# Loading the first columns of a weight from the scalar queue, and scheduling the output projection further behind its transposes

## The chip, the core and the metric

The kernel runs on one core of one Trainium2 chip. The metric is device time in microseconds (us), taken as the median of the runs. The profiled span is about 1.75 us shorter than the device time of the same execution (153.8 against 155.57), so spans are compared with spans only. Every timed run was also listed with its span and its granted TensorE clock: the share of full speed at which TensorE was allowed to run, averaged over the run.

A ratio below is the mean time of one kernel's fast runs over the mean of the other kernel's fast runs in the same rounds, so it is not quite the ratio of the medians that are quoted.

## The reference, cut to what matters

```python
xn = layernorm(x)                        # x: 1 x 2048 x 448, bf16
h  = silu(xn @ w1)                       # w1: 448 x 1792
ff = h @ w2                              # w2: 1792 x 448
q, k, v = split(xn @ wqkv)               # 16 heads of 28
# phi_q, phi_k: softmax of +/- (q @ w_phi), 56 features a head
o  = (phi_q @ (phi_k.T @ v)) / den
return x + o @ wo + ff
```

The kernel works on 16 tiles of 128 rows. At the start it needs a tile of `x`, its layer norm, its transpose, and the first columns of `w1`. At the end it needs the attention output `o` of each tile, transposed by a DMA, as the stationary operand of the product with `wo`.

## The kernel before: the parts that matter

Every operation is recorded first. A list scheduler in the kernel's Python then fixes the order on each engine, from modelled durations. Two kinds of numbers only steer that order: `lat` of a load, and `slack`, which makes an operation count as ready later than its inputs. Neither makes the chip wait. What the chip waits for are semaphores.

```python
            for d in o.deps:
                dd = ops[d]
                t = max(t, dd.end + lat(dd, o) + (o.slack if dd.eng != o.eng else 0.0))
```

The loads. All but `Wp` stand in the sync queue, in this order:

```python
        load(Wp[:], A_w_phi.rearrange("(g hl) d f -> (hl d) g f", g=G), "wphi", eng="act", lat=3000.0)
        load_x(0, 1)
        load_x(1, 2)
        load_x(2, 4)
        load_w1(0, 512, 3200.0)
        load_w1(512, 1024, 3200.0)
        load_x(4, 8)
        load_w1(1024, FF)
```

`load_w1` makes two transfers: 384 rows (384 KB for 512 columns, called the first piece of w1 below) and the last 128 rows (128 KB).

The first four tiles are normalized on VectorE and transposed by TensorE. Fixed chains keep their order:

```python
        chain("bnst0 bnag0 bnst1 bnag1 rstd0 xn0 rstd1 xn1 bnst2 bnag2 bnst3 bnag3 rstd2 xn2 rstd3 xn3 ev3".split())
        chain("ev0 ve2 ev1 ve3 ev2 silu_table".split())
        chain("tr0 tr1 tr2 tr3".split())
        # [...]
        for t, fs in ((0, head[:2]), (1, head[:2]), (0, head[2:3]), (1, head[2:3]), (2, head[:3]), (3, head[:3])):
            for f in fs:
                f[0](True, t * 128, t * 128 + 128)
```

`xn0`, tile 0's normalization, stands behind `bnst1`, the statistics of tile 1. `ev1`, ScalarE's copy of tile 1's transpose, stands behind `ve2`, tile 2's square root. So tile 1's operand waits for the load of tiles 2 and 3.

The end of the kernel:

```python
        def wo_fulls(q, ob, cs, st):
            P.cur_slack = 900.0
            for n in range(3):
                mm(ob, oT_sb[:, q, n + q % 2, :], wo_sb[:, q % 2, n, cs], st and n == 0, False, "wo_mm")
            P.cur_slack = 0.0
```

The softmax here doesn't subtract the row's maximum and nothing guards it: scores larger than these inputs give would overflow.

## Time and profile before

| | before |
|---|---|
| median of the first 3 runs | 153.57 us (153.53 to 153.88) |
| the profiled execution itself | 155.57 us, span 153.8 us, mean granted clock 0.989 |
| TensorE busy | 148.2 us, 96% of the span |

The profile is of an execution 2.0 us longer than the median.

The page of the kernel before: the span, the busy time of TensorE, its busy tenths in 40 slices and its granted clock in tenths.

```profile
span 153.8 us, 2800 instructions
PE 148.2 (96%) x1118; PEld 79.4 (52%) x1118; DVE 90.0 (59%) x171; ACT 72.6 (47%) x86; POOL 67.4 (44%) x76
PE   7599999999999999999999999999999999999993
PEclk9959999999999999999999999999999999999999
```

TensorE is full from the third slice on, but in that slice the clock was at half.

The chain of work that ended last in before, in order of time (start us, duration us, what; PE is TensorE, and L438 is the line of the helper through which its matmuls go):

```profile
2.20 5.12 DMA phT<-in_B_w_dram
7.32 0.14 issue
7.45 1.93 PE psum L438 x19
...
10.87 86.31 PE psum L438 x653
...
118.81 4.37 DMA vaug<-vaug
...
123.23 28.00 PE psum L438 x215
```

Read backwards, this execution hangs on TensorE, then on one transposed attention output (`vaug`), then on TensorE, and at the start on the first piece of w1, which is stored under the name `phT`: issued 2.20, landed 7.32.

The timeline of before at both places (start us, duration us, engine, line, what, and in brackets the idle time before it and what ended that):

```profile
3.87 0.59 DVE L563 BATCH_NORM_STATS2 st<-x_sb 128x6 f32<-128x448 bf16 x1
...
5.73 0.60 ACT L458 ACTIVATE xnT<-psum 128x512 bf16<-128x512 bf16 x1 [0.71 <-PE psum L453]
...
7.38 0.58 ACT L458 ACTIVATE xnT<-psum 128x512 bf16<-128x512 bf16 x1
...
7.45 1.93 PE L438 MATMUL psum<-xnT,phT 128*128 128x128 bf16 x19 [1.33 <-DMA phT<-in_B_w_dram]
...
123.23 0.74 PE L438 MATMUL psum<-wo_sb,vaug 128*128 128x448 bf16 x3 [0.22 <-DMA vaug<-vaug]
```

The first line is tile 1's statistics, the next two are the copies of tiles 0 and 1. Both copies were done before or soon after the first feed-forward matmul: only w1 was late.

### The profile page before, as it was taken

What the parts mean: (1) busy time and instruction counts of PE and PEld (TensorE: products, weight loads), DVE (VectorE), ACT (ScalarE), POOL (GpSimd) and SP (SyncE); (2) the same over time, 40 slices, a digit from 0 to 9 for tenths busy, and PEclk for the clock granted to TensorE, in tenths of its full rate; (3) what the DMA queues carried; (4) which work ended last, traced back from release to release, by engine and by line L of the source; (5) the groups of instructions that cost most, each with busy time, mean ns of one, the idle gap of its engine ahead of it and who ended that gap; (6) DMA issues with size and microseconds to landing.
All of it is one profiled execution on the core that took longest, in us unless ns stands there. A gap on an engine that the chain in (4) does not pass through costs nothing.

```text
span 153.8 us, 2800 instructions
## 1 busy us (share of the span) xinstructions
PE 148.2 (96%) x1118; PEld 79.4 (52%) x1118; DVE 90.0 (59%) x171; ACT 72.6 (47%) x86; POOL 67.4 (44%) x76
## 2 busy tenths in 40 slices
PE   7599999999999999999999999999999999999993
PEld 7497444446444556545434444445554455555482
DVE  1748888306019998897112521999973724474552
ACT  3452884676688669698555759784000000000000
POOL 7105564300014999999993000499997000000000
PEclk9959999999999999999999999999999999999999
DMA  5997554799940000000058311065899993144151
GB/s 90 320 387 285 112 105 81 91 240 280 238 137 0 4 0 0 9 0 0 4 114 161 66 34 38 0 122 98 171 124 191 207 199 68 39 124 124 36 155 64
DMA packets 44206, 17.38 MB, mean 113 GB/s; under 512 B 36640, under 2 KB 43808, under 8 KB 44192
## 3 DMA queue, kind: packets, MB, share of 16 engines
q1 hardware_dynamic: 41568, 15.44, 45.3%
q10 hardware_dynamic: 2624, 1.75, 3.8%
q8 instruction: 9, 0.15, 0.4%
q14 instruction: 5, 0.04, 0.1%
HBM read 6.56 MB, written 1.84 MB: 55 GB/s over the span
## 4 chain that ended last, share of the span: by engine, by line
PE 91%; DMA 6%; SPq 1%; issue 0%; DVE 0%
PE psum L438 90%; DMA phT<-in_B_w_dram 3%; DMA vaug<-vaug 3%; SPq L499 1%; PE psum L453 1%; DVE x_sb L776 0%
## 5 line engine op out<-in xcount | busy, mean ns | idle before, releaser
L438 PE MATMUL psum<-xnT,phT 128*128 128x512 bf16 (+2 forms) x278 | 49.2, 346 | 1.3 <-DMA phT<-in_B_w_dram 1.3
L438 PE MATMUL psum<-w_sb,hT 128*128 128x448 bf16 (+1 forms) x238 | 48.6, 342 | 0.0
L458 ACT ACTIVATE hT<-psum 128x1024 bf16<-128x1024 f32 x28 | 27.9, 1025 | 18.8 <-PE psum L438 18.8
L706 POOL TENSOR_TENSOR RA<-Ek_sb,Rec 128x896 bf16<-128x896 bf16 x16 | 26.6, 1700 | 16.3 <-DVE Rec L674 16.3
L438 PEld LDWEIGHTS psum<-xnT,phT 128*128 128x128 bf16 (+1 forms) x278 | 21.1, 102 | 21.6 <-issue 4.7
L438 PEld LDWEIGHTS psum<-w_sb,hT 128*128 128x128 bf16 x238 | 22.2, 98 | 17.4 <-issue 0.6
L673 DVE TENSOR_REDUCE Rec<-Ek_sb 128x64 f32<-128x1792 bf16 x12 | 23.7, 1978 | 12.0 <-ACT Ek_sb L458 12.0
L458 ACT ACTIVATE Ek_sb<-psum 128x896 bf16<-128x896 f32 x24 | 20.4, 927 | 5.0 <-PE psum L438 2.3
L681 POOL TENSOR_TENSOR Ek_sb<-Ek_sb,Rec 128x896 bf16<-128x896 bf16 x8 | 13.3, 1698 | 5.7 <-DVE Rec L674 5.6
L753 DVE TENSOR_SCALAR den<-psum 128x16 f32<-128x16 f32 x16 | 2.7, 171 | 19.6 <-PE psum L438 19.6
L438 PE MATMUL psum<-wv,xnT 128*128 128x448 bf16 (+1 forms) x64 | 13.5, 352 | 0.0
L438 PE MATMUL psum<-Wk,xnT 128*128 128x448 bf16 (+1 forms) x64 | 13.5, 353 | 0.0
L681 POOL TENSOR_TENSOR phT<-phT,Rec 128x896 bf16<-128x896 bf16 x8 | 13.3, 1706 | 0.0
L438 PE MATMUL psum<-Wq,xnT 128*128 128x448 bf16 (+1 forms) x64 | 12.5, 353 | 0.0
L438 PE MATMUL psum<-wo_sb,vaug 128*128 128x448 bf16 (+1 forms) x51 | 11.7, 342 | 0.2 <-DMA vaug<-vaug 0.2
L563 DVE BATCH_NORM_STATS2 st<-x_sb 128x6 f32<-128x448 bf16 x16 | 9.6, 602 | 3.7 <-DMA x_sb<-in_A_x_dram 3.7
L776 DVE TENSOR_TENSOR x_sb<-psum,x_sb 128x448 bf16<-128x448 f32 (+1 forms) x13 | 7.1, 583 | 5.9 <-PE psum L438 5.8
L760 DVE TENSOR_TENSOR vaug<-psum,rden 128x448 bf16<-128x448 f32 x16 | 10.0, 624 | 0.8 <-DVE rden L755 0.2
L578 DVE TENSOR_SCALAR RA<-x_sb,mv,rstd 128x384 bf16<-128x384 bf16 (+2 forms) x28 | 8.8, 350 | 2.7 <-POOL rstd L574 2.6
L674 DVE RECIPROCAL Rec<-Rec 128x64 f32<-128x64 f32 x16 | 8.7, 546 | 0.3
L673 DVE TENSOR_REDUCE Rec<-phT 128x64 f32<-128x1792 bf16 x4 | 8.0, 1990 | 0.9 <-ACT phT L458 0.9
L572 POOL TENSOR_SCALAR ve<-mv 128x1 f32<-128x1 f32 x12 | 2.6, 217 | 13.2 <-DVE mv L564 13.2
(49 smaller groups left out, 118.2 us busy)
## 6 DMA issues: line engine op xcount, KB each, us to landing
out_dram<-x_sb ACTq DMA_DIRECT2D x15, 112.0 KB, 2.6
w_sb<-in_B_w_dram SPq DMA_DIRECT2D x1, 1568.0 KB, 8.0
x_sb<-in_A_x_dram SPq DMA_DIRECT2D x3, 448.0 KB, 7.4
phT<-in_B_w_dram SPq DMA_DIRECT2D x2, 384.0 KB, 5.3
wo_sb<-in_A_wo_dram SPq DMA_DIRECT2D x2, 336.0 KB, 4.0
phT<-in_B_w_dram SPq DMA_DIRECT2D x1, 576.0 KB, 7.1
wv<-in_A_wqkv_dram SPq DMA_DIRECT2D x1, 336.0 KB, 7.2
phT<-in_B_w_dram SPq DMA_DIRECT2D x2, 128.0 KB, 5.2
```

Of the source, the lines that this page charges most:

```text
L438: r = e.matmul(dst, lhsT, rhs, start=st, stop=sp, skip_group_check=True)
L458: P.op("act", d_act(n), lambda e: e.activation(dst, src, func, scale=scale), reads=[src], writes=[dst], table=table, name=name, **keys)
L563: P.op("dve", 590, lambda e: e.bn_stats(st6[:, t, :], xs), reads=[xs], writes=[st6[:, t, :]], name=f"bnst{t}", okeys_w=["ln"])
L572: P.op("pool", 200, lambda e: e.tensor_scalar(ve[:, t:t + 1], mv[:, t, 1:2], EPS_LN, None, ALU.add), reads=[mv[:, t, 1:2]], writes=[ve[:, ...
L578: P.op("dve", dur, lambda e: e.tensor_scalar(dst, x_sb[:, t, c0:c1], mv[:, t, 0:1], rstd[:, t:t + 1], ALU.subtract, ALU.mult), reads=[xs, ...
L673: P.op("dve", 1985, lambda e: e.tensor_reduce(R2, E4, AXL.X, ALU.add), reads=[E4], writes=[R2], name="Ssum")
L674: P.op("dve", 555, lambda e: e.reciprocal(R2, R2), reads=[R2], writes=[R2], name="Rrec")
L681: P.op("pool", 1700, lambda e: e.tensor_tensor(E3, E3, Rk[:, :, None].broadcast_to([128, 32, DH]), ALU.mult), reads=[E3, Rk], writes=[E3], ...
L706: P.op("pool", 1700, lambda e: e.tensor_tensor(dst, Eq, Rq.rearrange("p (c j) -> p c j", c=CC)[:, :, :, None].broadcast_to([128, CC, 4, DH ...
L753: P.op("dve", 190, lambda e: e.tensor_scalar(den[:, uq, :], U3[:, :, DH], EPS_DEN, None, ALU.add), reads=[U3[:, :, DH]], writes=[den[:, uq ...
L760: P.op("dve", 620, lambda e: e.tensor_tensor(o3, U3[:, :, 0:DH], rden[:, uq, :, None].broadcast_to([128, H, DH]), ALU.mult), reads=[U3[:, ...
L776: P.op("dve", d_dve(cs.stop - cs.start), lambda e: e.tensor_tensor(res[:, cs], ob, addend[:, cs], ALU.add), reads=[ob, addend[:, cs]], wri ...
```

## The change

Its intent is to let TensorE start earlier, by issuing the first 512 columns of w1 from the otherwise idle scalar queue, and to keep TensorE from reaching a `wo` product before its transposed operand has landed.

```diff
+        load_w1(0, 512, 2000.0, "act")
         load_x(2, 4)
-        load_w1(0, 512, 3200.0)
-        load_w1(512, 1024, 3200.0)
+        load_w1(512, 1024, 2500.0)
         load_x(4, 8)
[... load_rows4 and load_w1 pass eng on ...]
         def wo_fulls(q, ob, cs, st):
-            P.cur_slack = 900.0
+            P.cur_slack = 1500.0
[... the same in finish_tile ...]
```

On TensorE the static order changes in two separate places. In the head, 9 instead of 6 feed-forward matmuls stand before tile 3's transposes. After 116 us, `wo` products stand behind more `w2` products.

More of the change, by code (lines that the diff above doesn't have):

```diff
@@ L502, in load_x, with load_rows4, load_w1 @@
             load(x_sb[:, t0:t1, :], xt[:, t0:t1, :], f"x{t0}")
-        def load_rows4(dst, src, c0, c1, name, lat=1700.0):
-            load(dst[:, 0:3, :], src[0:KF, c0:c1].rearrange("(k p) f -> p k f", p=128), name, lat=lat)
-            load(dst[:, 3, :], src[D - 128:D, c0:c1], name, lat=lat)
-        def load_w1(c0, c1, lat=1700.0):
-            load_rows4(w1_sb[:, :, c0:c1], B_w1, c0, c1, "w1", lat)
+        def load_rows4(dst, src, c0, c1, name, lat=1700.0, eng="sp"):
+            load(dst[:, 0:3, :], src[0:KF, c0:c1].rearrange("(k p) f -> p k f", p=128), name, lat=lat, eng=eng)
+            load(dst[:, 3, :], src[D - 128:D, c0:c1], name, lat=lat, eng=eng)
+        def load_w1(c0, c1, lat=1700.0, eng="sp"):
+            load_rows4(w1_sb[:, :, c0:c1], B_w1, c0, c1, "w1", lat, eng)
         load(Wp[:], A_w_phi.rearrange("(g hl) d f -> (hl d) g f", g=G), "wphi", eng="act", lat=3000.0)
@@ L790, in finish_tile @@
                 wo_fulls(q, ob, cs, t < NYT)
-                P.cur_slack = 900.0
+                P.cur_slack = 1500.0
                 pe_mms([wo_rem(q, ob, slice(0, 128), cs)], "wo_mm")
```

## The prediction

> **What bounds it now.** TensorE. The page gives PE 148.2 us busy of a 153.8 us span; the chain of waits puts 90% on the matmul helper and ends in matmuls from 7.45 us to 151.23 us, then one addition and one store. So only time before 7.45 us, and TensorE gaps after it, can be won.
>
> The head, from the timeline: warm-up matmuls end at 4.9, the transposes of tiles 0 and 1 at 6.12, then TensorE idles 1.33 us until the first w1 piece (issued 2.20, landed 7.32) lets the feed-forward start at 7.45. Tile 0's operand was ready at 6.33. The narrow windows show the clock at 1.0 until 7.75, at 0.5 from 7.75 to about 11.2, then 1.0: 7 to 8 matmuls per 0.5 us when slow, 13 afterwards. The Trainium skill, "TensorE: Matmul & The Clock Gate" (HAM clock gate), says that a too idle window of about 3.4 us halves the clock for the next; this trace agrees (3.41 us at 0.5 after that gap).
>
> Near the end the waits show one stall on the transposed attention output: at 123.23 TensorE starts about 0.4 us later than the 0.19 us spacing of its neighbours would have it.
>
> **What the change does.** It adds and removes no work. (1) The first 512 columns of w1 (384 + 128 KB) leave the sync queue (issued 2.20 and 2.68) for the scalar queue, behind w_phi's issue, which ended at 1.22; I expect 1.25 to 2.1, about 0.95 us earlier. (A 1.28 us table load on ScalarE starts there too; I expect the issue not to wait for its end.) Everything behind on the sync queue is issued 0.9 to 1.0 us earlier. (2) New latencies and a larger slack reorder the static schedule: wo's products wait 0.6 us longer in the model.
>
> **How much is on the critical path.** Not 0.95 us. The skill, "DMA: Bandwidth & Descriptors" (Issuing engines are not separate DMA queues), says that a second issuer saves only issue time, since all share the same 16 engines. From 4.5 us on they carry 300 to 400 GB/s here; between 3.0 and 4.5 us only 72 to 222, which the earlier issue can fill. But w1 now shares with x tiles 2 and 3 (landed 6.27) and the next w1 piece instead of following alone. I estimate the first piece at 6.7 (6.2 to 7.3), x tiles 2 and 3 unchanged or up to 0.3 late.
>
> Then a second gate shows. Tile 1's copy on ScalarE stands behind tile 2's square root, which waits for x tiles 2 and 3: it ran 7.38 to 7.96. Tile 0's 12 matmuls would be done by about 7.6, and tile 1's start near 8.2 instead of 8.65. Gain 0.2 to 0.6 us. If the added work before 7.75 us keeps the clock at full speed (30%), about 1 us more. The slack removes up to 0.4 us near 123 us, less what the new order costs elsewhere; I count 0.2.
>
> **Predicted time.** 152.8 us, 151.8 to 153.6 (8 in 10): 0.5% faster. Over 2% faster: 3%; within 2%: 95%; over 2% slower: 2%.
>
> **What would show it.** Right: two w1 issues on the scalar queue before 2.2 us; first feed-forward matmul between 6.4 and 7.2, then a short gap before tile 1; later stages shifted by the same amount, equal in length; no wait on the transposed output near 123 us. The clock window after 7.75 us tells whether the larger gain came.
>
> **What would make it wrong.** The scalar issue waits for the table load (issue at 2.75): w1 lands no earlier, gain near zero or a loss of 0.5 us. x tiles 2 and 3 land a microsecond late. The clock gate stays open: 151.5. The new static order brings a new stall after 116 us.

## The result

After takes 153.41 us (153.30 to 153.60, 5 runs), before 153.56 us (153.33 to 153.88, 5 runs). The ratio is 0.999, 95% interval 0.9975 to 1.0005: no difference that this measurement can tell from zero. The time lies inside the predicted range, but the forecast gain of 0.8 us does not exist.

The two profiles are not of the same kind. After's execution ran at full clock, as did all its runs (0.998 or more). The page of after:

```profile
span 151.6 us, 2800 instructions
PE 147.0 (97%) x1118; PEld 78.3 (52%) x1118; DVE 90.1 (59%) x171; ACT 72.6 (48%) x86; POOL 67.4 (44%) x76
PE   7799999999999999999999999999999999999993
PEclk9999999999999999999999999999999999999999
```

The spans, 153.8 and 151.6 us, suggest a gain of 2.2 us. The timed runs say that this is the difference between two executions, not between two kernels. The chain of after:

```profile
1.27 2.96 DMA x_sb<-in_A_x_dram
...
6.35 0.61 ACT xnT L458
6.96 0.04 issue
7.00 0.84 PE psum L438 x12
7.84 0.01 issue
7.85 0.56 PE psum L438 x7
...
95.32 53.64 PE psum L438 x386
```

The DMA at the end, 118.81 to 123.18 in before, is gone: TensorE runs from 95.32 to 148.96 in one piece. At the start the chain no longer hangs on w1. It hangs on an x load (tile 1, issued 1.27, landed 4.23), through the normalization and the copy of tile 0. The timeline of after shows this step by step:

```profile
1.25 1.28 ACT L458 ACT_TABLE_LOAD   x1 [1.25 <-PEq L1020]
1.31 0.99 ACTq L499 DMA_DIRECT2D phT<-in_B_w_dram  x2
...
4.26 0.63 DVE L563 BATCH_NORM_STATS2 st<-x_sb 128x6 f32<-128x448 bf16 x1 [0.30 <-DMA x_sb<-in_A_x_dram]
...
6.35 0.60 ACT L458 ACTIVATE xnT<-psum 128x512 bf16<-128x512 bf16 x1 [0.92 <-PE psum L453]
...
7.00 1.41 PE L438 MATMUL psum<-xnT,phT 128*128 128x128 bf16 x19 [0.44 <-ACT xnT L458]
...
7.22 0.58 ACT L458 ACTIVATE xnT<-psum 128x512 bf16<-128x512 bf16 x1
...
120.77 1.87 PE L438 MATMUL psum<-wo_sb,vaug 128*128 128x448 bf16 x9
```

The scalar queue issued w1 at 1.31, as predicted, during the table load. Tile 1's statistics waited for their load and began at 4.26, where before began at 3.87. Tile 0's copy then ran at 6.35 instead of 5.73. The last line has nine `wo` products without a wait.

### The profile page after: what moved, and what is told of

Same layout as the page of the kernel before. It is cut to its first block, busy times and chain, and to the rows that moved or that the text cites. A ratio compares the mean times of both kernels' runs of the same rounds, so it can differ in the third digit from the quotient of the medians.

```text
span 151.6 us, 2800 instructions
## 1 busy us (share of the span) xinstructions
PE 147.0 (97%) x1118; PEld 78.3 (52%) x1118; DVE 90.1 (59%) x171; ACT 72.6 (48%) x86; POOL 67.4 (44%) x76
## 4 chain that ended last, share of the span: by engine, by line
PE 94%; DMA 2%; DVE 1%; ACT 0%; SPq 0%; issue 0%
PE psum L438 93%; DMA x_sb<-in_A_x_dram 2%; PE psum L453 1%; DVE st L563 0%; ACT xnT L458 0%; SPq L499 0%; DVE RA L578 0%; DVE x_sb L776 0%; DVE mv L564 0%; DVE rstd L569 0%
## 5 line engine op out<-in xcount | busy, mean ns | idle before, releaser
L438 PE MATMUL psum<-xnT,phT 128*128 128x512 bf16 (+2 forms) x278 | 48.1, 338 | 0.4 <-ACT xnT L458 0.4
L438 PEld LDWEIGHTS psum<-xnT,phT 128*128 128x128 bf16 (+1 forms) x278 | 19.8, 97 | 20.9 <-issue 3.2
L458 ACT ACTIVATE phT<-psum 128x896 bf16<-128x896 f32 x8 | 7.0, 930 | 2.9 <-PE psum L438 2.9
```

Source lines behind the costliest of these rows:

```text
L438: r = e.matmul(dst, lhsT, rhs, start=st, stop=sp, skip_group_check=True)
L458: P.op("act", d_act(n), lambda e: e.activation(dst, src, func, scale=scale), reads=[src], writes=[dst], table=table, name=name, **keys)
```

## The experiments

Two theories were set against each other, for each half of the change.

- Head: either the earlier w1 starts TensorE earlier (the prediction), or w1's earlier packets delay the x tiles, so that the start hangs on them and nothing is won.
- End: either the stall near 122 us is worth its 0.4 to 0.7 us, or it moves elsewhere.

There were fourteen runs of kernels, in four batches on four chips. Each batch has its own 11 timings of before on its chip. All are within 2% of before but w1 held, which has a single timing, whose state is unknown. The results of all, with ratios to before of the same batch:

| kernel | median us (lowest to highest) | before's median | ratio (95%) |
|---|---|---|---|
| before again | 153.76 (153.35 to 154.16) | 153.66 | 1.0013 (0.9984 to 1.0043) |
| queue alone | 154.17 (153.66 to 155.15) | 153.66 | 1.0048 (1.0016 to 1.0081) |
| slack alone | 153.19 (152.90 to 153.53) | 153.66 | 0.9982 (0.9958 to 1.0005) |
| after, tile 0 first | 153.95 (153.85 to 154.24) | 153.66 | 1.0032 (1.0010 to 1.0053) |
| after again | 153.65 (153.41 to 153.89) | 154.02 | 0.9993 (0.9960 to 1.0027) |
| x tile 1, then w1, on scalar | 153.22 (152.99 to 153.44) | 154.02 | 0.9967 (0.9933 to 1.0001) |
| only x tile 1 on scalar | 153.20 (153.14 to 155.19) | 154.02 | 0.9990 (0.9937 to 1.0043) |
| w1 held back | 158.03 (one look) | 154.02 | |
| order alone | 153.68 (153.47 to 155.44) | 153.76 | 1.0018 (0.9976 to 1.0060) |
| queue, old order | 154.16 (153.67 to 155.21) | 153.76 | 1.0028 (0.9999 to 1.0057) |
| slack alone, again | 153.06 (152.93 to 153.23) | 153.76 | 0.9963 (0.9937 to 0.9989) |
| x tile 1, then w1, again | 153.23 (153.02 to 153.49) | 153.76 | 0.9975 (0.9948 to 1.0002) |
| after, third | 153.59 (153.24 to 154.74) | 153.64 | 1.0017 (0.9987 to 1.0048) |
| slack alone, third | 153.30 (152.95 to 153.74) | 153.64 | 0.9989 (0.9968 to 1.0009) |

And the head of every profile (us): when the last of a load's 16 landing records came, and when three feed-forward matmuls started. The 13th is the first that needs tile 1 (tile 0 has 12). The 72nd is the last of the head's small ones. A missing number means that the order of the head differs there. In slack alone, third, the second 128 KB piece of w1 came late (9.63), which held up the 72nd.

| profile | x tile 0 | x tile 1 | x tiles 2, 3 | w1 first piece | x tiles 4 to 7 | 1st | 13th | 72nd | clock |
|---|---|---|---|---|---|---|---|---|---|
| before | 3.09 | 3.54 | 6.27 | 7.32 | 10.20 | 7.45 | 8.43 | 13.48 | half from 7.76 |
| before again | 3.06 | 3.54 | 5.41 | 6.44 | 10.09 | 6.58 | 7.26 | 11.02 | full |
| slack alone | 3.17 | 3.62 | 5.79 | 6.88 | 10.13 | 7.01 | 7.68 | 11.42 | full |
| slack alone, again | 3.12 | 3.56 | 5.79 | 6.82 | 10.38 | 6.95 | 7.62 | 11.36 | full |
| slack alone, third | 3.15 | 3.59 | 5.59 | 6.64 | 10.78 | 6.78 | 7.44 | 12.03 | full |
| order alone | 3.15 | 4.10 | 5.92 | 7.00 | 10.39 | 7.14 | 8.31 | 13.17 | half from 7.24 |
| after | 3.10 | 4.23 | 6.11 | 5.49 | 8.93 | 7.00 | 7.85 | 11.61 | full |
| after again | 3.06 | 4.11 | 6.22 | 5.20 | 8.89 | 6.67 | 7.96 | 11.71 | full |
| after, third | 3.08 | 3.96 | 6.12 | 5.15 | 8.74 | 6.72 | 7.85 | 11.61 | full |
| queue alone | 3.11 | 4.40 | 6.57 | 6.28 | 9.26 | 7.12 | 8.31 | 12.06 | full |
| queue, old order | 3.05 | 4.53 | 6.57 | 5.53 | 9.20 | 7.30 | 8.55 | 12.92 | no record before 9.86, slow spacing |
| after, tile 0 first | 3.03 | 4.04 | 6.28 | 5.09 | 8.93 | 6.41 | | | full |
| x tile 1, then w1 | 3.44 | 3.60 | 5.03 | 6.02 | 9.31 | 7.02 | 7.69 | 11.43 | full |
| x tile 1, then w1, again | 3.42 | 3.58 | 4.48 | 5.46 | 8.94 | 7.00 | 7.66 | 11.40 | full |
| only x tile 1 on scalar | 3.43 | 3.60 | 4.49 | 6.38 | 9.44 | 7.02 | 7.92 | 11.68 | full |
| w1 held back | 3.10 | 3.73 | 5.57 | 12.07 | 8.91 | 6.80 | | | half from 13.24 |

The clock column leaves out the start. Up to the first clock record (3.83 to 6.45 us in all profiles but two) the matmuls stand 107 ns apart, as in a stretch at half clock; after it they stand 56 ns apart. The PEclk digits of a page and the listed clock leave that start out too. In queue, old order, the first record comes only at 9.86 us and the spacing is 107 ns until then, although the run is listed at clock 1.0. So a listed 1.0 does not rule out a slow head. (The other profile, only x tile 1 on scalar, has no record; its spacing becomes 56 ns near 4.2 us.)

Everything between the head and the end is alike. From the 72nd of these matmuls to the 386th matmul from the end, every profile takes 83.71 to 83.74 us, except the control (84.27) and w1 held (83.94). The last 386 matmuls take 53.62 us in every profile with the new slack and 54.02 to 54.36 us in every one with the old. So the profiles differ only in the head, in the end, and in one stall of the control that is shown below.

### The control: before once more

No edit.

> The unchanged kernel before, as a control. Theory 1 (the profile that the prediction was built on caught an execution in which the clock fell to 0.5 from 7.75 to 11.2 us, and most executions keep it): ratio 1.000 within 0.003; runs listed with clock 1.00 have a span near 151.8 us, any run listed with about 0.99 one near 153.8 us; a profile at clock 1.00 has the first feed-forward matmul near 7.4 us and shows no half-speed stretch after it. Rival (the clock of before falls in every execution): all runs have clock 0.99 and span near 153.8 us.

Measured: ratio 1.0013. All 17 runs of before in this batch were at clock 0.999 or more, with spans from 151.0 to 152.4 us. Over the four batches all 50 timed runs of before are listed at 0.998 or more. The profile on which the prediction stood was the exception. Busy time by engine in stretches of before, then of the control (stretch and length in us; busy us and instruction count of PE, PEld, DVE, ACT, POOL, which are TensorE, its weight loads, VectorE, ScalarE and GpSimd; granted clock; DMA share; GB/s):

```profile
4.34:7.75 3.41, 1.65 (x23) 1.18 (x22) 2.60 (x10) 1.48 (x5) 0.00 (x0) 1.00 1.01 339
7.75:11.17 3.42, 3.42 (x36) 3.42 (x34) 1.29 (x6) 1.75 (x4) 0.00 (x0) 0.50 1.04 385
```

```profile
3.99:7.40 3.41, 2.35 (x36) 1.86 (x34) 3.20 (x12) 2.16 (x6) 0.34 (x1) 1.00 1.01 345
7.40:10.81 3.41, 3.41 (x65) 3.41 (x63) 1.75 (x6) 2.13 (x4) 0.00 (x0) 1.00 1.02 376
```

In the same length of time the control issued 65 matmuls where the half-speed execution issued 36. Two things were different in the stretch before: the control's w1 landed at 6.44 instead of 7.32, and TensorE was busy for 2.35 us instead of 1.65. So at full clock the first matmul with before's loads comes at 6.58 to 7.01 us, not 7.45, and tile 1's at 7.26 to 7.68, not 8.43 (the control and the three profiles of slack alone, whose head is the same). One number of the expectation missed: 6.58 instead of 7.4.

The control shows a second gate, which was hidden in the slow profile. Its chain:

```profile
4.21 5.88 DMA x_sb<-in_A_x_dram
10.12 0.64 DVE st L563
...
20.06 75.21 PE psum L438 x560
...
116.87 4.73 DMA vaug<-vaug
121.65 28.01 PE psum L438 x215
```

TensorE started early there, then stood until 20.06 us (0.77 us between two starts at 19.3, where its neighbours have about 0.21). The matmul at 20.06 needs the DMA transpose of the normalized tiles 6 and 7, which landed at 19.93, at the end of a chain that began with tiles 4 to 7 of x at 10.09. (The profile puts this wait down to a ScalarE copy that ended then too, but in slack alone the same matmul started before that copy ended.) Nothing in that chain was late: in slack alone tiles 4 to 7 landed at 10.13 and the transpose at 19.81, and TensorE came to the same matmul at 19.94 without a wait. So, with the loads as before, a still earlier head is given back at this place: the control's 72nd matmul came 0.40 us before slack alone's, and its next stretch was 0.53 us longer. This stall was seen in one profile only.

### Each half alone

Queue alone is the diff above with slack left at 900.

> The first half of the change alone: w1's first 512 columns from the scalar queue, with the new modelled latencies, slack left at 900. Theory 1 (the head's gain is real but small because the x tiles land later): span 0.1 to 0.4 us under before at clock 1.00, first feed-forward matmul at 7.0 us waiting for the copy of tile 0, not for w1. Rival (the head gains nothing and all 0.15 us comes from the slack): span equal to before within 0.1 us.

Measured: slower by an interval that excludes 1, 1.0048 (1.0016 to 1.0081). The theory had expected a small gain, so even this sign was missed; the mechanism it named is what the profile shows. The timeline of queue alone:

```profile
4.43 0.63 DVE L563 BATCH_NORM_STATS2 st<-x_sb 128x6 f32<-128x448 bf16 x1 [0.45 <-DMA x_sb<-in_A_x_dram]
...
6.60 0.63 DVE L563 BATCH_NORM_STATS2 st<-x_sb 128x6 f32<-128x448 bf16 x1 [0.34 <-DMA x_sb<-in_A_x_dram]
...
7.12 0.84 PE L438 MATMUL psum<-xnT,phT 128*128 128x128 bf16 x12 [0.41 <-ACT xnT L458]
...
8.31 0.40 PE L438 MATMUL psum<-xnT,phT 128*128 128x128 bf16 x4 [0.35 <-ACT xnT L458]
```

VectorE waits twice for x, TensorE twice for ScalarE's copies, and never for w1, which had landed at 6.28. The stall at the end is there too (0.64 us between two starts at 121.23).

Slack alone:

```diff
-            P.cur_slack = 900.0     # wo_fulls and finish_tile
+            P.cur_slack = 1500.0
```

> The second half alone: slack of wo's products 1500, all loads as before. As predicted: the 0.4 us stall near 123 us is gone and the span is 0.2 to 0.4 us under before at clock 1.00. Rival (in an execution with full clock TensorE reaches that place later in terms of the transfer, or the stall moves): no difference, within 0.1 us.

Measured: 0.9982. The interval just includes 1, so it was run again beside the candidate below:

> The slack half alone again, to make its interval narrower: 0.3 to 0.7 us under before (ratio 0.995 to 0.998), the size of the stall near 121 us that three profiles with the old slack show (0.38, 0.46 and 0.72 us beyond the usual spacing). Rival: no difference.

Measured: 0.9963 (0.9937 to 0.9989), which excludes 1. The end of the chain of slack alone has no DMA in it:

```profile
95.16 53.64 PE psum L438 x386
148.80 0.02 issue
148.82 0.39 DVE x_sb L776
```

The 386 matmuls take 53.64 us without the stall. In before the same stretch took 21.61 + 4.37 + 0.05 + 28.00 = 54.03 us, in queue alone 54.1 us, in the control 54.4 us. So the stall is worth 0.4 to 0.7 us in the profiles. The mean times of the three comparisons (the third follows below) differ by 0.30, 0.61 and 0.20 us (before less slack alone). Only the second of the three intervals excludes 1. The stronger evidence is that all three have one sign, and that the stall is in all five profiles with the old slack and in none of the eleven with the new.

### Order or transfers?

The queue half changes both TensorE's order in the head and the transfers. Order alone has the two latencies 2000 and 2500, all loads on the sync queue, slack 900.

> Only the two modelled latencies of the change (2000 and 2500), with every load still on the sync queue and slack 900: TensorE's head gets after's order (9 matmuls before tile 3's transposes, not 6), the transfers are before's. Theory (the transfers made the queue half slower): ratio to before 1.000 within 0.002, landings as before (tile 1 at 3.5 to 3.7 us). Rival (the new order of the head made it slower): slower by 0.3 to 0.5 us, ratio near 1.003.

Measured: 1.0018 (0.9976 to 1.0060). That is with its profiled run of 155.44 us, which had the half-speed stretch; the other five runs have 153.47 to 153.77, before's median is 153.76. So the order by itself costs nothing that shows. One landing missed: tile 1's last record came at 4.10, although its 15th of 16 came at 3.59. One late part of the 16 is enough for that.

Queue with the old order has w1 on the scalar queue and both latencies at 3200, which gives exactly before's order on TensorE.

> The counterpart: w1's first 512 columns on the scalar queue, both modelled latencies back at 3200, which gives exactly before's order on TensorE; slack 900. Theory: the time of queue_only, 0.2 to 0.7 us over before, with tile 1's load at 4.0 to 4.4 us and tiles 2 and 3 at 6.1 to 6.6. Rival: equal to before within 0.1 us.

Measured: 1.0028 (0.9999 to 1.0057), median 0.4 us over before, with tile 1 at 4.53 and tiles 2 and 3 at 6.57. The interval just includes 1, and the profiled run (155.21 us) had TensorE at half speed up to 9.86 us. The means differ by 0.50 us with that run and by 0.33 us without it. Together with queue alone, which has the same transfers and the order of order alone, this points to the transfers. Whether later tiles also make such slow heads more frequent was not tested.

### Are the x tiles late because w1 runs between them?

What the transfer engines moved between 3 and 4 us, in after and then in slack alone, which has before's loads (q1 is the sync queue, q10 the scalar queue; packets, MB, share of 16 engines):

```profile
q10 hardware_dynamic: 207, 0.21, 69.7%
q1 hardware_dynamic: 59, 0.04, 19.5%
```

```profile
q1 hardware_dynamic: 103, 0.14, 97.9%
```

In after, w1 had most of this microsecond, and the sync queue with the x tiles moved less than a third of what it moved without w1 beside it. In the six profiles with the change's loads it moved 32 to 59 KB in that microsecond, in the six with all of w1 on the sync queue and x in its old place 90 to 179 KB.

In the first of three attempts w1 was held back until x tile 1 had landed:

```diff
-            load(dst[:, 0:3, :], ..., eng=eng)
+            load(dst[:, 0:3, :], ..., eng=eng, after=[x_sb[:, 1, :]] if eng == "act" else ())
```

> A look only at transfers: the whole change, but the scalar queue's first w1 load waits until tile 1's x load has landed (the static order of TensorE's head moves too, so the time is no verdict). Theory (w1's packets in between are what made tile 1 and tiles 2 and 3 late): tile 1 lands again at 3.5 to 3.6 us, tiles 2 and 3 at 5.4 to 5.8, and the first w1 piece at 7 us or later. Rival (tile 1 was late by chance, or because of the earlier issue of the sync queue's other loads): tile 1 still lands at 4.0 us or later.

Measured: tile 1 at 3.73, tiles 2 and 3 at 5.57. That is back near the old values (the unheld 128 KB piece of w1 still ran among them, which may be the 0.1 to 0.2 us missing). W1, issued at 3.75 on a nearly empty scalar queue, landed at 12.07. The transfer engines already had the sync queue's later loads: this load of w1 moved its first packet of data only at 7.50. Timeline, then stretches of this kernel:

```profile
12.11 1.07 PE L438 MATMUL psum<-xnT,phT 128*128 128x128 bf16 x16 [2.17 <-DMA phT<-in_B_w_dram]
```

```profile
9.83:13.24 3.41, 1.24 (x23) 1.13 (x21) 3.03 (x11) 0.71 (x2) 2.17 (x6) 1.00 1.08 394
13.24:16.65 3.41, 3.41 (x33) 3.04 (x32) 2.84 (x10) 0.00 (x0) 1.77 (x5) 0.50 1.09 222
```

The 2.17 us wait left TensorE 1.24 us busy in one stretch of 3.41 us, and the clock was halved in the next, as in the first profile of before.

Second, tile 0 was taken off tile 1's load:

```diff
-        chain("bnst0 bnag0 bnst1 bnag1 rstd0 xn0 rstd1 xn1 ...
+        chain("bnst0 bnag0 rstd0 xn0 bnst1 bnag1 rstd1 xn1 ...
```

> The whole change, and tile 0's normalization moved ahead of tile 1's statistics on VectorE, so that tile 0 no longer waits for tile 1's load, which landed at 4.23 us after and at 3.54 us before. The static order of TensorE moves with it: tile 1's transposes now follow tile 0's matmuls. Theory 1 (tile 0's path behind tile 1's load is what gates the start): first feed-forward matmul near 6.1 us instead of 7.0, span up to 0.6 us under after. Rival (the next gate, tile 1's copy behind the load of x tiles 2 and 3, takes it all): first matmul earlier, but tile 1's matmuls still near 7.8 us or later, and the span as after within 0.1 us.

Measured: the first matmul came at 6.41, so tile 1's load had gated it, but tile 1's matmuls came only at 8.78 and the kernel was slower (1.0032). The rival was right about the next gate. This edit also put tile 1's square root behind tile 0's copy on ScalarE, so it is no clean measurement of that gate.

Third, tile 1 went to the head of the scalar queue, with w1 behind it and `Wp` last:

```diff
         load_x(0, 1)
-        load_x(1, 2)
+        load_x(1, 2, "act")
         load_w1(0, 512, 2000.0, "act")
+        load(Wp[:], ...)          # was first on the scalar queue
         load_x(2, 4)
```

> The whole change, with tile 1's x load put first on the scalar queue, w1's two loads behind it there, and the small w_phi load last; x tiles 2 and 3 are then second on the sync queue. Theory (after the change the x tiles gate the start, because w1's packets now run between theirs): tile 1 lands at 3.0 to 3.3 us instead of 4.0 to 4.4, the first feed-forward matmul comes near 6.3 us instead of 7.0, and the span is 0.5 to 1.0 us under after. Rival (w1 on a second ring slows the x tiles by the same amount wherever they stand): x tiles 2 and 3 still land at 6.1 us or later, tile 1's matmuls do not start before 7.8 us, and the time equals after within 0.2 us.

Beside it, the whole change again:

> The whole change again, beside the runs that follow and on their chip. If the two halves add up (queue alone +0.5 us, slack alone -0.3 to -0.45 us), the time is within 0.3 us of before, ratio 0.998 to 1.003, as when first measured. Landings: tile 1's load near 4.0 to 4.4 us, x tiles 2 and 3 at 6.1 to 6.6 us, first w1 piece at 5.1 to 6.3 us, no stall near 123 us.

Measured: 153.22 us against 153.65 us for after, in the same rounds. Tile 1 landed at 3.60, tiles 2 and 3 at 5.03, and tile 1's matmuls started at 7.69 instead of 7.96. The theory holds in sign, at half the size. The first matmul did not come at 6.3 but at 7.02, because two x loads started at once and tile 0 now landed at 3.44 instead of 3.06 to 3.10. Repeated beside slack alone:

> The candidate for a version that beats both, beside slack_only on one chip: 0.4 to 0.8 us under before, and 0 to 0.3 us under slack_only. If it equals slack_only within 0.1 us, then no placement of w1 on the scalar queue that was tried is worth anything by itself.

Measured: 153.23 against 153.06 us for slack alone. So this placement repairs what the change had broken and wins nothing on top.

Only x tile 1 on the scalar queue, w1 back in its old place:

> Slack 1500; w1 back on the sync queue behind all the x tiles that it stood behind before; only tile 1's small x load goes to the scalar queue, ahead of w_phi, so that every load on the sync queue is issued 0.47 us earlier in the old order. Theory (the order x before w1 is what matters, and issue time is worth having where it keeps that order): tile 1 lands near 3.1 us, x tiles 2 and 3 0.3 to 0.5 us earlier than before (5.0 to 5.8), w1 likewise (6.0 to 6.9), x tiles 4 to 7 near 9.7 instead of 10.1; span 0.3 to 0.5 us under slack_only, about 0.8 under before. Rival (transfers are limited by bytes, not by issue, so an earlier issue moves nothing): landings and time as slack_only within 0.1 us.

Measured: 153.14 to 153.38 us in five runs and 155.19 us in one, whose listed clock is 1.0 and whose profile was not kept; its cause is open. A slow head as in queue, old order, is one candidate. The expected 0.8 us under before was missed: the means differ by 0.2 us, or by 0.6 us without that run. Tiles 2 and 3 landed at 4.49, w1 at 6.38, both earlier as expected. But tile 0 was 0.3 us later, and the first matmul again came at 7.02.

### Does the queue half cost time with the new slack too?

> The whole change, beside slack_only on one chip for the first time. If moving w1 costs time also with the new slack: mean 0.2 to 0.6 us above slack_only's, spans 151.6 to 152.2 us. Rival (the two are equal and the difference seen so far is between batches): means within 0.15 us.

> The slack alone, beside the whole change: spans 151.1 to 151.8 us at full clock, ratio to before 0.996 to 0.998, and 0.2 to 0.6 us below the whole change. Rival: equal to the whole change within 0.15 us.

Measured: mean 153.68 us for the whole change and 153.32 us for slack alone, 0.37 us apart. Without the whole change's one run of 154.74 us it is 0.16 us. Slack alone's ratio, 0.9989, lies outside the expected 0.996 to 0.998. The sign agrees with the other batches. The size, 0.2 to 0.4 us, is at the edge of what these rounds resolve.

## Why the prediction was wrong

What was right: the issue on the scalar queue at 1.31 and 1.79 without waiting for the table load; a first matmul between 6.4 and 7.2; the copy of tile 1 as a gate; and the stall near 123 us, which the slack removes.

The steps that failed, in the prediction's words:

- "[...] tile 1's start near 8.2 instead of 8.65. Gain 0.2 to 0.6 us." Both ends were off. The base (8.43 by the table's count) was read from an execution with a late w1 and the clock at half. At full clock tile 1's matmuls start at 7.26 to 7.68 with the loads as before, and at 7.85 to 7.96 after. The term of +0.2 to +0.6 us gained is a loss: +0.2 to +0.4 us with the new slack, and 0.5 and 0.7 us (differences of means; 0.3 for the first without its half-speed run) where the queue half ran alone. In the profiles the 72nd matmul came at 11.61 to 11.71 in after and at 11.36 and 11.42 in two of slack alone's three (12.03 in the third, where a w1 piece was late).
- "Tile 0's operand was ready at 6.33." It was taken as fixed. It waits for tile 1's load, and that landed at 3.96 to 4.53 in all six profiles with the change's loads (after three times, queue alone, queue with the old order, tile 0 first), against 3.54 to 3.62 in five of six with w1 on the sync queue (4.10 in the sixth). And there was little to win: with the loads as before and full clock, in the control and slack alone, that operand was ready at 6.30 to 6.61 and w1 landed at 6.44 to 6.88, 0.1 to 0.5 us later, not 1.0 us as in the first profile. The prediction named the sharing of the engines, and even a delay of tiles 2 and 3, but did not follow tile 1's load through the chain on VectorE.
- "I estimate the first piece at 6.7 (6.2 to 7.3)." The change did more for w1 than predicted: 5.09 to 5.53 in five of six profiles. It was simply no longer what the start waited for.
- "If the added work before 7.75 us keeps the clock at full speed (30%), about 1 us more." The clock did stay up, but it stays up in before's timed runs too. That term compared an unusual execution with a usual one.
- The slack was counted as 0.2 us. It measured 0.2, 0.3 and 0.6 us, 0.4 on average.

So the small total, ratios of 0.999, 0.9993 and 1.0017, is a sum of two terms of opposite sign. The slack wins 0.2 to 0.6 us. The queue half loses about as much, because it lets w1 overtake the x tiles, on which two serial chains hang. That the time fell inside the predicted range is luck: before's own median, 153.57 us, lies inside it too. Slack alone is the best supported version: it was below before three times, once by an interval that excludes 1. That it also beats the whole change is likely but rests on one comparison in the same rounds.

What stays open: before's runs spread from 151.0 to 152.6 us of span at a listed clock of 0.998 or more. The landing of a load's last part (tiles 2 and 3: 5.41 or 6.27), the second gate at 20 us and a clock that rises late are candidates, but only profiles of several executions could tell.

## What to carry to other kernels

Look at whether the profiled execution is as long as the timed ones, and at its granted clock, before taking any gap from it as the base of a sum. Moving a load to a second queue can do more than issue it earlier: here it let w1 run among the loads that it used to stand behind. So follow each of those to what waits for it. When two edits come together and the total is near zero, run each alone.

## What the Trainium skill lacked or had wrong

- "DMA: Bandwidth & Descriptors", section Issuing engines are not separate DMA queues, says that issuing from several engines saves only the sequencer's issue time. It says that the transfers interleave, but not what that can cost: with w1 moved to the second queue, w1 landed about 1.5 us earlier (5.09 to 5.53 in five of six profiles, against 6.44 to 7.32) and x tile 1 about 0.6 us later. The page's section Queues, rings and completion order has a mechanism (an engine takes turns between queue rows, a packet at a time). The trace of after fits it in so far as both queues moved data between 3 and 4 us (207 and 59 packets). The trace of w1 held does not look like even turns: from 4.1 to 7.5 us the sync queue moved 744 packets and the scalar queue one, with w1's load issued there at 3.75. It landed 8.3 us after its issue, at 12.07. Why is open.
- "TensorE: Matmul & The Clock Gate", Part 1, puts the return to half clock after an idle window of about 3.4 us, without a measure of how idle, and its section Why this matters for your kernels advises against idle gaps over about 3 us. (For another kernel the page tells of frequent short idles, without a figure.) Here no gap over 2.4 us was needed. In stretches of 3.41 us counted from the first clock record, the clock was halved after 1.65 (before), 1.71 (order alone) and 1.24 us (w1 held) of TensorE busy time, and kept after 2.08 (slack alone, again), 2.15 (after again), 2.18 (w1 held) and 2.35 us (the control). The longest gap between matmul starts in the first of these was 1.55 us. On the way up it stayed at half after a stretch with 2.68 us busy (queue, old order, 3.03 to 6.44) and rose after one with 2.77 us (order alone, 0.41 to 3.83), one case each.
- No page that was read says outright whether a DMA issue waits behind a table load on the scalar queue. It does not here: issues at 1.31 and 1.79 us ran during a table load from 1.25 to 2.53 us.
